# A planner's costs for crossbar transposes beside loads, and the order that it makes, in an attention and gated feed-forward kernel

## The chip, the cores and the metric

The kernel runs on one core of one Trainium2 chip. The metric is the device time of one execution in microseconds (us), from the runs shown below. The engines that matter are TensorE (PE in the profile, with its weight loads as PEld), VectorE (DVE), ScalarE (ACT), GpSimd (POOL), which here only issues loads, and SyncE (SP), which issues crossbar transposes and stores.

## The reference

```python
def _attn_ref(q, k, v):                       # each 8 x 12 x 448 x 64
    scale = 1.0 / np.sqrt(q.shape[-1])
    scores = scale * np.matmul(q, k.transpose(0, 1, 3, 2))
    attn = np.maximum(scores, 0.0) ** 2 / S
    return np.matmul(attn, v)

def _moe_ref(x, w_gate, w_val, w_out):        # 3584 x 768; 768 x 1536 twice; 1536 x 768
    gate = np.maximum(x @ w_gate, 0.0)
    val = x @ w_val
    return gate * val @ w_out
```

The attention's heads are joined to a 3584 x 768 matrix, which is the feed-forward's `x`. Inputs and output are float32; the kernel computes in bfloat16.

## The kernel before

The work goes by batch (8, named b) and by group of four heads (3 to a batch, named g), 24 groups in all. A group's queries and keys are loaded to `raw`, its values to `vv`, both by POOL (L393, `dma_in`). They have to be transposed to `qkT`. For the first two batches TensorE does that (L508, L515, L555). For the other 18 groups VectorE copies `raw` into `perm`, of which there is one buffer (L579), and SP issues two crossbar transposes `perm` to `qkT` (L585), a pair for each group. Then TensorE forms the scores (L653), ScalarE or VectorE applies relu (L664, L666) and square (L676, L678), and TensorE multiplies by the values (L695). The results of a batch are `xT`.

The feed-forward of the first two batches is plain (L760 for gate and value). From the third batch on, two batches go together by Strassen's scheme with seven products for eight (L869), and the output products do so for all batches (L984). Their sums are formed on VectorE and ScalarE (among them L816 to L822, L897, L935, L974). Stores go out from SP, the last ones from ACT too (L956).

While TensorE waits for the first loads it runs products whose result nobody reads ("filler", L1138).

The order of every engine's queue is made by the class `Planner` and the function `plan` when the program is built. The planner keeps a time for each engine, each buffer and two DMA queues (loads, transposes), and repeatedly lets the operation start that it thinks can start first. Each engine then executes its queue in order, waiting by semaphore where an input is late. The planner's costs therefore change no instruction, only the order and which of ScalarE and VectorE does an operation that both can do. Three strings hold the result of a search: `PE_ORDER` (how attention, in lower case, and feed-forward, in upper case, are merged on TensorE), `LOAD_ORDER` (POOL's loads) and `AHEAD` (by how many tenths of a microsecond each operation of the other engines is preferred or put back).

The costs of the two DMA queues are these. A load arrives `TO_LOAD` after its issue, needs its own work (`op.load`) at full rate, and ends `LOADED` after that. A pair of transposes likewise has `TO_TURN`, `TURN` and `TURNED`. While both queues hold something, each gets half of the rate (L135 to L164, `advance` and `transfer`). An operation of TensorE or another engine that needs a transposed tile is kept `LATE[0]` behind its landing; a buffer that a DMA reads is free `LATE[1]` behind its end. Operations of VectorE and ScalarE that read a load are kept `MARGIN` behind it.

Of the kernel before, what the change touches and what calls it, by code (L numbers as in the profile page):

```python
# [15 lines left out]
class Res:  # L16


    def __init__(self, n):
        self.free = {i: 0.0 for i in range(n)}  # L20
# [21 lines left out]
class Op:  # L42


    def __init__(self, engs, emit, deps=(), alloc=(), reads=(), mode=None, grp=None):
        self.engs, self.emit = engs, emit
        self.deps, self.alloc, self.reads = list(deps), list(alloc), list(reads)
        self.mode, self.grp = mode, grp
        self.load = self.land = 0.0
        self.kind = self.behind = None  # L50
        self.xbar = 0
        self.start = self.end = self.eng = None
        for b in self.reads:
            b.readers += 1


class Planner:
    NOUT = 8
    SWITCH = 0.1
    BIAS = 0.2  # L60
    MARGIN = 1.0
# [43 lines left out]
    def ready(self, op):  # L105
        r = 0.0
        for d in op.deps:
            if d.end is None:
                return None
            if d.eng != "PE" or "PE" not in op.engs:  # L110
                r = max(r, d.end + (self.LATE[0] if d.xbar else 0.0))
        for b in op.alloc:
            p = b.pick(self.now(op))
            if p is None:
                return None
            r = max(r, p[0])
        return r

    def best(self, op):
# [4 lines left out]
        for e, (occ, busy) in op.engs.items():  # L124
            if e in ("DVE", "ACT"):
                r = max([r] + [d.end + self.MARGIN for d in op.deps if d.load])
            s = max(r, self.t.get(e, 0.0))
# [4 lines left out]
                c = (f, s, e)  # L132
        return c[1], c[2], r

    def advance(self, t):  # L135

        a, b = self.queues
        while self.dma_t < t and (a or b):
            rate = 0.5 if a and b else 1.0
            d = min(min(q[0][1] for q in (a, b) if q) / rate, t - self.dma_t)  # L140
            self.dma_t += d
            for q, post in ((a, self.LOADED), (b, self.TURNED)):
                if q:
                    q[0][1] -= d * rate
                    if q[0][1] < 1e-6:
                        q.pop(0)[0].end = self.dma_t + post
        self.dma_t = max(self.dma_t, t)

    def transfer(self, queue, op, arrival, work):


        self.advance(arrival)
        self.queues[queue].append([op, work])
        a, b = ([list(x) for x in q] for q in self.queues)
        t = self.dma_t
        while a or b:
            rate = 0.5 if a and b else 1.0
            d = min(q[0][1] for q in (a, b) if q) / rate
            t += d
            for q, post in ((a, self.LOADED), (b, self.TURNED)):  # L160
                if q:
                    q[0][1] -= d * rate
                    if q[0][1] < 1e-6:
                        q.pop(0)[0].end = t + post  # L164

    def commit(self, op, s, e):
        assert op.behind is None or op.behind.start is not None
# [28 lines left out]


PE_ORDER = (
    'aadccabacbcadafgabaedabbafecaaCacaFFABAacbaAAieadbbJJIIbaaIHAFGahebccbJJHcaaHFICBDgaadbCFbaEDABBBabfeBANCccLBa'
    'aIIGDAABegcdaBIAEbbaHACCgbbdaDDFcaaAAAbgbdAAdaACBbaAAhcbbAaabBCBAaaCBAebbaCBbaaEAGBBcDBFAEBAADCBAGAAHAEBBCBAAB'  # L200
    'DfaAADaaCABAcBBABaaACAAacbabDADAEEAABABADAabEDDBACEAAACCbaBABABbbCBaaABDAbbEAAabAGAebaAACEAabEEFABfbBEgaAAabhc'
    'BBcgbCCaDAecdABbaaAAAAaaacBAADaaDBDACAAEBCAcbDAHBAGAABAAAacAGAAaabBAAAAABAAAbbaCAAIAAAbbaDAAbcCAAAHBAHacAAFbaB'
    'DEAgbaABCCBACBABBDABAedCBAbaaAFCAAAAAeaaaICcaAAAbaABAaaaaBBcaaCEIACaBEJAKAADBAACABAAABAAAAAABAAAAAABAAAADADHCB'
    'DCBICHABCFBHACAFEBEHBABCAEGBBDBBDCCECAAAGBABBABBBCGEAABBCBCCBABBABBBA'
)
LOAD_ORDER = (
    'aaaabacebaacbacaabaaabadhcegaadeedabaaacahbgcabgeefdaddafccaabdacadmacehaadadmaaiabbdfhiadcaaabccgladdigaaabcb'
    'aaaabaa'
)
AHEAD = (  # L210
    'mlmmmolklollknklnlmomknomlmmmmnlllomnollmmomkommlmkmmmmjmkknqkkhnmnliilnnommmokoljkkopnmnojokmioinklrnkohplrmi'
    'hjolnponoeilomskljrjkunmqpnmjjnmjijjmomolsmokiiijnhpotkioksohoolopnjirmompnjppplhmnjqgjpoqqmnjkmpljmlkklkoqkoj'
    'noookqplkjlllgnoqntlloopmpopnmjlnoomonlmpnqmqklmlnkkknojpsonpgmnmkkhnmommnpjmlmjnlhompplnmnookmlmoqkkkkolmoopj'
    'ooplpmnoomomnnolmmmmkmmmmmmlmmmnnknnnpllmlonlonlmmkgnmqlkpmniuilqnlliruojriqkoosmnpqophgpnitnjinonoqpnplnmmmll'
    'loknokmlmmjnpopnojmnmljnliqimnenkoojmkgjdoonlmnnrtnorhogrmppnijllliomrorkigpjnpjkmqoonohloqlmqohpnpmpmikklooin'
    'ltlvnnnomkmmunipomhnnmjjgmmmphgjnloilsogplmomplqiolkkkqhnmkngojmojkllmnohmjjkpklnkrnkkklomlilmnkjknjknokqlnlll'
    'kjjlpnmrljklmmniqnpqilknmlklmnllolojonnimnpliljkionjoilklkiimmkrloonniolnlnkmnonnklmlklkmlnnnmmmmmmmmmmmmmmmmm'
    'mmomnmklkkolmlommolnnnnmlmloljmlpikogimnolpolqjjnimlngpijlpmkonknlmjleklpsjnoqnqlqkmilrsmmoomjojmjhppsjrpppllq'
    'horhmnknqrpknjpmpnokjjppnhilpmhomiphpmpojqokkkpoonkoihjkmojnljklipnqlnnksnklmkirqmpmklhgknllfrlgqkjknmlfjnrrmp'
    'slmrmnnnikmonninkjmmmqjlikpqqmnjohpijopklkn'  # L220
)

# [75 lines left out]
def kernel(  # L298
# [28 lines left out]
    OH = d_model // 2  # L327
# [21 lines left out]
    wo = pool.tile([128, 2, 2, FH, OH], BF16, name="wo")  # L349
# [39 lines left out]
    others, pool_ops = [], []  # L389


    def dma_in(dst, src, n_desc, us, deps=(), alloc=()):
        op = Op({"POOL": (0.5 + 0.0004 * n_desc,) * 2}, lambda: nc.gpsimd.dma_start(out=dst(), in_=src),  # L393
                deps=deps, alloc=alloc)
        op.load = us
        pool_ops.append(op)
        return op

    wg_op, wv_op, wo_op = {}, {}, {}

    def load_gv(m0, m1):

        cols = slice(m0 * 128, m1 * 128)
        for ops, sb, w in ((wg_op, wg, moe_w_gate), (wv_op, wv, moe_w_val)):
            src = w.rearrange("(kd p) f -> p kd f", p=128)
            op = dma_in(lambda sb=sb: sb[:, :, cols], src[:, :, cols], 768,
                        1.075 * (m1 - m0) + (0.0 if wv_op or sb is wv else 0.65))
            for m in range(m0, m1):
                ops[m] = op

    def load_out(par, hf):
        src = moe_w_out.rearrange("(g par p) m -> p par g m", p=128, par=2)
        wo_op[(par, hf)] = dma_in(lambda: wo[:, par, hf], src[:, par, :, hf * OH:(hf + 1) * OH], 768, 3.0)

    class Quad:
        pass
# [730 lines left out]
    def load_quad(b, g):  # L1147
        load_qk(b, g)
        load_v(b, g)
# [3 lines left out]
    for x in Planner.ORDER:  # L1153
        if x in "VL":
            for g in range(NQ):
                load_v(0, g) if x == "V" else late_q(g)
        elif x in quad_of:
            load_quad(*quad_of[x])
        elif x in out_of:
            load_out(*out_of[x])  # L1160
        elif x == "6":
            load_gv(1, 2)
        elif x == "0" and "6" in Planner.ORDER:
            load_gv(0, 1)
        else:
            load_gv(2 * int(x), 2 * int(x) + 2)
# [83 lines left out]
```

## Time and profile before

| | |
|---|---|
| timed runs, us | 407.9, 406.82, 404.08 (median 406.82) |
| profiled execution, us | 403.85 |
| its span, first to last instruction, us | 402.1 |
| granted TensorE clock | 0.998 |
| TensorE busy | 390.4 us, 97% |
| VectorE, ScalarE, GpSimd busy | 81%, 66%, 19% |
| HBM read, written | 47.19 MB, 11.01 MB |

The profile shows one execution. Its busy times say how full each engine is; the waits of TensorE say what it stood for; the chain that ended last says which work set the end; the timeline shows single places. Wherever a view gives "to landing", it is the time from the issue of a DMA to the last of its data. Times in a view count from the span's start.

### The profile page before, as it was taken

What the parts mean: (1) busy time and instruction counts of PE and PEld (TensorE: products, weight loads), DVE (VectorE), ACT (ScalarE), POOL (GpSimd) and SP (SyncE); (2) the same over time, 40 slices, a digit from 0 to 9 for tenths busy, and PEclk for the clock granted to TensorE, in tenths of its full rate; (3) what the DMA queues carried; (4) which work ended last, traced back from release to release, by engine and by line L of the source; (5) the groups of instructions that cost most, each with busy time, mean ns of one, the idle gap of its engine ahead of it and who ended that gap; (6) DMA issues with size and microseconds to landing.
All of it is one profiled execution on the core that took longest, in us unless ns stands there. A gap on an engine that the chain in (4) does not pass through costs nothing.

```text
span 402.1 us, 8702 instructions
## 1 busy us (share of the span) xinstructions
PE 390.4 (97%) x3472; PEld 209.0 (52%) x3472; DVE 325.2 (81%) x570; ACT 267.1 (66%) x395; POOL 75.7 (19%) x121
## 2 busy tenths in 40 slices
PE   7899998999999999999999999999999999999995
PEld 4577554455455554444455544444455555555563
DVE  4998784999899869988998978998889858768661
ACT  3888884768987637957859874588688853233231
POOL 8845541032202110212102220310100000000000
PEclk9999999999999999999999999999999999999999
DMA  8999999987999585266567993761513320000245
GB/s 112 191 197 199 199 182 198 151 124 98 116 156 166 120 152 82 41 93 102 81 101 136 195 196 50 111 91 30 76 36 82 80 59 0 2 0 2 60 120 138
DMA packets 77305, 43.44 MB, mean 108 GB/s; under 512 B 40912, under 2 KB 77264, under 8 KB 77264
## 3 DMA queue, kind: packets, MB, share of 16 engines
q0 software_dynamic: 34896, 23.60, 42.2%
q1 hardware_dynamic: 42048, 18.89, 25.4%
q8 instruction: 27, 0.44, 0.4%
q10 hardware_dynamic: 320, 0.39, 0.3%
q14 instruction: 14, 0.11, 0.1%
HBM read 47.19 MB, written 11.01 MB: 145 GB/s over the span
## 4 chain that ended last, share of the span: by engine, by line
PE 88%; DMA 9%; issue 1%; POOL 1%; ACT 1%; DVE 0%; SPq 0%; DVEq 0%; POOLq 0%
PE ps L869 35%; PE ps L984 24%; PE ps L760 12%; PE ps L653 9%; PE ps L695 7%; DMA qkT<-perm 6%; DMA gvT<-in_k_dram 1%; DMA vv<-in_v_dram 1%; POOL gvT L393 1%; PE ps L555 1%; ACT at L664 0%; DVE g L935 0%; ACT qkT L481 0%; DVE o L974 0%; PE ps L1138 0%
## 5 line engine op out<-in xcount | busy, mean ns | idle before, releaser
L664 ACT ACTIVATE at<-ps 128x896 bf16<-128x896 f32 (+4 forms) x124 | 108.2, 903 | 23.6 <-PE ps L653 23.3
L816 ACT COPY f<-ps 128x448 f32<-128x448 f32 x97 | 51.2, 532 | 49.1 <-PE ps L869 38.7
L678 DVE TENSOR_TENSOR at<-at 128x896 bf16<-128x896 bf16 (+4 forms) x108 | 64.0, 608 | 10.3 <-ACT at L664 8.9
L676 ACT ACTIVATE at<-at 128x896 bf16<-128x896 bf16 (+2 forms) x63 | 59.1, 952 | 1.7 <-DVE at L666 0.8
L666 DVE TENSOR_SCALAR at<-ps 128x896 bf16<-128x896 f32 (+3 forms) x47 | 50.6, 1076 | 4.1 <-PE ps L653 2.8
L653 PE MATMUL ps<-qkT 64*64 64x448 bf16 (+2 forms) x756 | 49.5, 337 | 1.8 <-DMA qkT<-perm 1.7
L869 PE MATMUL ps<-sx,wv 128*128 128x448 bf16 x216 | 51.1, 353 | 0.0
L869 PE MATMUL ps<-xT,gvT 128*128 128x448 bf16 x216 | 50.4, 353 | 0.0
L869 PE MATMUL ps<-xT,wg 128*128 128x448 bf16 x216 | 49.4, 353 | 0.8 <-DVE g L935 0.8
L393 POOL DMA_DIRECT2D vv<-in_v_dram x44 | 26.6, 609 | 119.0 <-PE ps L653 105.3
L869 PEld LDWEIGHTS <-gvT 128*128 128x128 bf16 x324 | 30.9, 98 | 30.7 <-issue 2.9
L984 PEld LDWEIGHTS <-sh 128*128 128x128 bf16 x312 | 29.8, 98 | 22.2 <-issue 1.9
L984 PEld LDWEIGHTS <-hT 128*128 128x128 bf16 x270 | 25.3, 98 | 20.6 <-issue 4.2
L984 PE MATMUL ps<-wo,hT 128*128 128x384 bf16 x192 | 35.6, 326 | 0.0
L695 PE MATMUL ps<-at,vv 64*64 64x448 bf16 (+2 forms) x700 | 34.0, 328 | 0.8 <-ACT at L664 0.5
L974 DVE SCALAR_TENSOR_TENSOR o<-ps,f 128x384 f32<-128x384 f32 x41 | 22.6, 555 | 13.9 <-PE ps L984 8.2
L653 PEld LDWEIGHTS <-qkT 64*64 64x64 bf16 x756 | 19.1, 105 | 26.1 <-issue 20.1
L818 ACT ACTIVATE f<-ps 128x384 f32<-128x384 f32 x39 | 19.1, 492 | 19.8 <-PE ps L984 17.8
L869 PEld LDWEIGHTS <-wg 128*128 128x128 bf16 x216 | 20.6, 98 | 21.4 <-issue 3.2
L760 PE MATMUL ps<-xT,wg 128*128 128x448 bf16 (+2 forms) x180 | 31.5, 316 | 0.0
L760 PE MATMUL ps<-xT,wv 128*128 128x448 bf16 (+2 forms) x180 | 31.3, 316 | 0.0
L869 PEld LDWEIGHTS <-wv 128*128 128x128 bf16 x216 | 20.2, 98 | 21.3 <-issue 3.7
(71 smaller groups left out, 489.9 us busy)
## 6 DMA issues: line engine op xcount, KB each, us to landing
out_dram<-o SPq DMA_DIRECT2D x108, 96.0 KB, 2.2
vv<-in_v_dram POOLq DMA_DIRECT2D x44, 112.0 KB, 5.3
raw<-in_k_dram POOLq DMA_DIRECT2D x18, 224.0 KB, 4.9
raw<-in_q_dram POOLq DMA_DIRECT2D x18, 224.0 KB, 6.1
wo<-in_moe_w_out_dram POOLq DMA_DIRECT2D x4, 576.0 KB, 15.1
wv<-in_moe_w_val_dram POOLq DMA_DIRECT2D x5, 384.0 KB, 9.7
wg<-in_moe_w_gate_dram POOLq DMA_DIRECT2D x5, 384.0 KB, 9.6
gvT<-in_k_dram POOLq DMA_DIRECT2D x6, 224.0 KB, 7.6
```

Of the source, the lines that this page charges most:

```text
L393: op = Op({"POOL": (0.5 + 0.0004 * n_desc,) * 2}, lambda: nc.gpsimd.dma_start(out=dst(), in_=src), deps=deps, alloc=alloc)
L653: nc.tensor.matmul(banks()[64 * j:64 * j + 64, z, h2], lhsT=self.k_of(j, h2, k), rhs=self.q_of(j, h2), start=True, stop=True)
L664: nc.scalar.activation(self.at_of(i, m), banks(), AF.Relu)
L666: nc.vector.tensor_scalar_max(self.at_of(i, m), banks(), 0.0)
L676: nc.scalar.activation(a, a, AF.Square)
L678: nc.vector.tensor_tensor(a, a, a, ALU.mult)
L695: nc.tensor.matmul(ps[64 * h2:64 * h2 + 64, ps2.idx + j, :n], lhsT=st.v_of(j, h2, c), rhs=self.at_of(c)[64 * j:64 * j + 64, 0, h2], start= ...
L760: nc.tensor.matmul(ps[:, pb.idx, z * n:(z + 1) * n], lhsT=w[:, kd, fc], rhs=xT_t[xbuf[b].idx][:, kd, cols], start=(kd == 0), stop=(kd == K ...
L816: nc.scalar.copy(dst, src)
L869: nc.tensor.matmul(ps[:, pb.idx, :S], lhsT=w(g)[:, fc], rhs=rhs, start=start and g == 0, stop=stop and g == KH - 1, skip_group_check=True)
L974: op = Op({"DVE": V384}, lambda: nc.vector.scalar_tensor_tensor(o_t[ob.idx], ps[:, pb.idx, :OH], float(out_scale), f_t[fb.idx][:, :OH], AL ...
L984: nc.tensor.matmul(ps[:, pb.idx, :OH], lhsT=lhs(kf), rhs=rhs(kf), start=start and kf == 0, stop=kf == FH - 1, skip_group_check=True)
```

## The change

Four things in the planner, and the three strings.

- Loads and transposes that are under way together no longer get half each. Each load has a `share`, the part of the rate that a transpose gets beside it: 0.25 for queries, keys and the gate and value weights, 0.19 for the output weights, 0.5 for values.
- The six constants of the two DMA queues are set anew.
- What waits for a transposed tile is kept 2.0 instead of 1.0 us behind its planned landing, and TensorE, which was not kept off a load, is kept 0.3 us behind it; `MARGIN` goes from 1.0 to 1.5.
- `advance` and the look-ahead in `transfer` are merged into `flow`.

```diff
-    MARGIN = 1.0
-    LATE = (1.0, 1.0)
-    TO_LOAD, LOADED = 2.25, 0.8
-    TO_TURN, TURNED, TURN = 1.8, 0.55, 4.05
+    MARGIN = 1.5
+    LATE = (2.0, 1.0, 0.3)
+    TO_LOAD, LOADED = 2.35, 0.95
+    TO_TURN, TURNED, TURN = 1.7, 0.8, 3.65
...
-                r = max(r, d.end + (self.LATE[0] if d.xbar else 0.0))
+                r = max(r, d.end + (self.LATE[0] if d.xbar else self.LATE[2] if d.load else 0.0))
...
-            rate = 0.5 if a and b else 1.0
...
+    def rates(self, a, b):
+        if not (a and b):
+            return 1.0, 1.0
+        share = a[0][0].share
+        return 1.0 - share, share
+
+    def flow(self, a, b, t, until):
+        while t < until and (a or b):
+            rates = self.rates(a, b)
+            d = min([q[0][1] / r for q, r in zip((a, b), rates) if q] + [until - t])
+            t += d
+            for q, r, post in zip((a, b), rates, (self.LOADED, self.TURNED)):
+                if q:
+                    q[0][1] -= d * r
                     if q[0][1] < 1e-6:
                         q.pop(0)[0].end = t + post
+        return t
...
-    def dma_in(dst, src, n_desc, us, deps=(), alloc=()):
+    def dma_in(dst, src, n_desc, us, deps=(), alloc=(), share=0.25):
...
-        wo_op[(par, hf)] = dma_in(..., 768, 3.0)
+        wo_op[(par, hf)] = dma_in(..., 768, 3.0, share=0.19)
...
-            st.v_ops.append(dma_in(lambda j=j: st.vv()[64 * j:64 * j + 64], src, 128, 0.58,
+            st.v_ops.append(dma_in(lambda j=j: st.vv()[64 * j:64 * j + 64], src, 128, 0.58, share=0.5,
```

The strings begin like this, before and after; they differ over most of `AHEAD`, the first four rows of `PE_ORDER` and the second half of `LOAD_ORDER`'s first row.

```diff
-    'aadccabacbcadafgabaedabbafecaaCacaFFABAacbaAAieadbbJJIIbaaIHAFGahebccbJJHcaaHFICBDgaadbCFbaEDABBBabfeBANCccLBa'
+    'aaceccaacbcbacaeibbeccabaaecabAAacaFAccACaaabgcbaaNKJKATAHaaaJCICcebeJEEIbbFbaaGADFafabBABEabaBBAAabfeAKTLabKK'
...
-    'aaaabacebaacbacaabaaabadhcegaadeedabaaacahbgcabgeefdaddafccaabdacadmacehaadadmaaiabbdfhiadcaaabccgladdigaaabcb'
+    'aaaabacebaacbacaaeccbaaidceokbdacgeeafafiaegeahcdgdfdcacabdddbddaalllacacccaaalaiccbddagaabddahdeacanlcahjbhca'
```

Both programs have the same number of instructions of each kind that computes on TensorE except the filler (3472 and 3471 products with it), the same 117 loads, 36 transposes and 112 stores.

More of the change, by code (lines that the diff above doesn't have):

```diff
@@ L48, in __init__ @@
         self.mode, self.grp = mode, grp
-        self.load = self.land = 0.0
+        self.load = self.land = self.share = 0.0
         self.kind = self.behind = None
@@ L133, in best, with transfer @@
         return c[1], c[2], r
-    def advance(self, t):
-        a, b = self.queues
-        while self.dma_t < t and (a or b):
-            rate = 0.5 if a and b else 1.0
-            d = min(min(q[0][1] for q in (a, b) if q) / rate, t - self.dma_t)
-            self.dma_t += d
-            for q, post in ((a, self.LOADED), (b, self.TURNED)):
-                if q:
[L144 to L162, printed above, removed]
+    def rates(self, a, b):
[9 more added lines that the diff above has]
+            for q, r, post in zip((a, b), rates, (self.LOADED, self.TURNED)):
+                if q:
+                    q[0][1] -= d * r
                     if q[0][1] < 1e-6:
                         q.pop(0)[0].end = t + post
+        return t
+    def transfer(self, queue, op, arrival, work):
+        self.dma_t = max(self.flow(*self.queues, self.dma_t, arrival), arrival, self.dma_t)
+        self.queues[queue].append([op, work])
+        self.flow(*([list(x) for x in q] for q in self.queues), self.dma_t, 1e9)
     def commit(self, op, s, e):
@@ L198 @@
 PE_ORDER = (
-    'aadccabacbcadafgabaedabbafecaaCacaFFABAacbaAAieadbbJJIIbaaIHAFGahebccbJJHcaaHFICBDgaadbCFbaEDABBBabfeBANCccLBa'
[L200 to L203, printed above, removed]
+    'aaceccaacbcbacaeibbeccabaaecabAAacaFAccACaaabgcbaaNKJKATAHaaaJCICcebeJEEIbbFbaaGADFafabBABEabaBBAAabfeAKTLabKK'
+    'CCGbaCDCAhecddHBBbbaDGACafbdaDDbaaFCAAbgbdAAacACBbaAAhcbbCaabABBbaDAAAebbaCcaaBIABCBcBABEEBAADCBAGAAHAEBBCBAAB'
+    'DfaAADaaCABAcBBABaaACBAacbabDAAFCAACBCFCHBAEBCcBAAACbaAACAGAabbBABaaBCADAecbEACAaAFebaBACEAabEEFABfaFgaaABbdiA'
+    'caCeaGBABBecdCAcbaAAAABfabaAEKADBAQAAEAAACBAAAbaDBAbbBDABAdaGCAAaabAAECAaBABBAAbaAIBAAbbaDAAbcAAJBCBAHAAFacBFA'
+    'CbaACBACAAgbaAECEACBAedCAAbaaAFCAAAAAeaaaICcaAAbaAABAaaaaBBcbaCJEACaBEJAKAADBAACABAAABCBBBACBCDCBAABAAAADADHCB'
     'DCBICHABCFBHACAFEBEHBABCAEGBBDBBDCCECAAAGBABBABBBCGEAABBCBCCBABBABBBA'
@@ L206 @@
 LOAD_ORDER = (
-    'aaaabacebaacbacaabaaabadhcegaadeedabaaacahbgcabgeefdaddafccaabdacadmacehaadadmaaiabbdfhiadcaaabccgladdigaaabcb'
-    'aaaabaa'
+    'aaaabacebaacbacaaeccbaaidceokbdacgeeafafiaegeahcdgdfdcacabdddbddaalllacacccaaalaiccbddagaabddahdeacanlcahjbhca'
+    'bdaabba'
 )
 AHEAD = (
-    'mlmmmolklollknklnlmomknomlmmmmnlllomnollmmomkommlmkmmmmjmkknqkkhnmnliilnnommmokoljkkopnmnojokmioinklrnkohplrmi'
-    'hjolnponoeilomskljrjkunmqpnmjjnmjijjmomolsmokiiijnhpotkioksohoolopnjirmompnjppplhmnjqgjpoqqmnjkmpljmlkklkoqkoj'
@@ L218 @@
-    'mmomnmklkkolmlommolnnnnmlmloljmlpikogimnolpolqjjnimlngpijlpmkonknlmjleklpsjnoqnqlqkmilrsmmoomjojmjhppsjrpppllq'
-    'horhmnknqrpknjpmpnokjjppnhilpmhomiphpmpojqokkkpoonkoihjkmojnljklipnqlnnksnklmkirqmpmklhgknllfrlgqkjknmlfjnrrmp'
+    'mlmmmolklollknkknkmplknmkjnnnmolnlmmnqlkmoqokonmjkmkmokimmkloohjrnlghglokjjklmmqngmhtlhprneoficpkmjjsfnnpwrtpg'
+    'arogqkpqrainsvngkgjgjzorsopgfnlrljmjoprmpskjjdbhgmmttnkmrlwpellhjpnjkqpqrlnlqlskbktfsijmkppnnjgkqllpmfhrkrlloh'
+    'qtorjsllojjfkgpprlrhkmnppqlqoljlpmlnnrlooorlohholmjnlpofrwqmnfloogmisphjnnnhijlkqilojnokqkiomoorllqohglslmmmhn'
@@ new lines @@
+    'smlowookpgijmqkqmpjjrflkinkjiimhqpqommkljnnonompjslgpppjhornftieqplmirwlkthrihsurmosnrjfnmgvnhjnsrqoslhomntmol'
+    'mvliqeknljmkmqsqlhmpsilnjklimmapnrqlnmdjgokqqnnorpigtjqitsoomkggjihpntqtqnenkpkiiuoposrepoqlnthjmkplplkkkkmsio'
+    'irqvpnimlemgqspnnnbtukjkinnqjhgkkmqcisldokjnmqknkmklklofqnlpfnknqhlmknomgljilsiknjsnijlipknjmmpkjnrjlmqepmnflh'
+    'ghknornoimjpoljkpmoqjiorpofnlplnnkrbmqpgompihkkkisqinkijffhlqpurmqpovfmgmgnnoorlompkoljpnnlqomlkopskhoihmkmnok'
+    'onoiooemgipikpjimfknjomqmoipontjlkopgooljjlpmrjkifmhohpdjloliqokpmrligmhsufqrtosfrhrggpronqqkkmjmmlsqqlqtqoooq'
@@ L220 @@
+    'gmqikmklrspkmjrmonpihjponiinpmhmogphpmpnjqmklkoonlipgilmkmjnkjingpnqkmojsnklmkjrqmpmklhgknllfrlgqkjknmlfjnrrmp'
     'slmrmnnnikmonninkjmmmqjlikpqqmnjohpijopklkn'
@@ L389 @@
     others, pool_ops = [], []
-    def dma_in(dst, src, n_desc, us, deps=(), alloc=()):
+    def dma_in(dst, src, n_desc, us, deps=(), alloc=(), share=0.25):
         op = Op({"POOL": (0.5 + 0.0004 * n_desc,) * 2}, lambda: nc.gpsimd.dma_start(out=dst(), in_=src),
                 deps=deps, alloc=alloc)
-        op.load = us
+        op.load, op.share = us, share
         pool_ops.append(op)
@@ L412, in load_out @@
         src = moe_w_out.rearrange("(g par p) m -> p par g m", p=128, par=2)
-        wo_op[(par, hf)] = dma_in(lambda: wo[:, par, hf], src[:, par, :, hf * OH:(hf + 1) * OH], 768, 3.0)
+        wo_op[(par, hf)] = dma_in(lambda: wo[:, par, hf], src[:, par, :, hf * OH:(hf + 1) * OH], 768, 3.0, share=0.19)
     class Quad:
```

5 lines of the change are left out of this document (removed).

## Prediction, made before the changed kernel ran

> **What bounds the kernel now.** I read the page's busy times first, then TensorE's waits, then the chain that ended last, and last the timeline at the two places where the chain leaves TensorE.
>
> ```profile
> PE 390.4 (97%) x3472; PEld 209.0 (52%) x3472; DVE 325.2 (81%) x570; ACT 267.1 (66%) x395; POOL 75.7 (19%) x121
> ...
> PE 88%; DMA 9%; issue 1%; POOL 1%; ACT 1%; DVE 0%; SPq 0%; DVEq 0%; POOLq 0%
> ```
>
> TensorE is busy for 390.4 of 402.1 us. Of the 11.7 us left, some 4.5 lie behind its last product (rows below). A change of order adds or removes no product of the result, so it can work only on the idle time, on the filler products and on changes of matrix shape.
>
> ```profile
> PE ps L653 <- DMA qkT<-perm: 1.7, 1, 1.7
> PE ps L1138 <- DVE woT L1125: 1.4, 1, 1.4
> PE ps L869 <- DVE g L935: 0.8, 1, 0.8
> PE ps L508 <- DMA gvT<-in_q_dram: 0.8, 2, 0.4
> PE ps L555 <- issue: 0.6, 1, 0.6
> PE ps L515 <- issue: 0.6, 1, 0.6
> ```
>
> These are TensorE's own waits. The first is a wait for a crossbar transpose and is the target of the change; the third will turn out to be a transpose too. The 1.4 us is the start of the program, the rest belongs to the first 35 us.
>
> ```profile
> 51.67 14.19 DMA qkT<-perm
> 65.91 0.38 PE ps L653 x4
> ...
> 231.53 9.19 DMA qkT<-perm
> 240.90 0.48 issue
> 241.38 0.63 DVE g L935
> 242.05 1.29 PE ps L869 x6
> ...
> 325.45 44.29 PE ps L869 x234
> ...
> 372.26 25.36 PE ps L984 x156
> 397.65 0.56 DVE o L974
> ```
>
> This is the chain in order of time (start, us, what). It leaves TensorE for a transpose twice. From 325 us on it is products alone, at 44.29/234 = 0.189 us for 448 columns and 25.36/156 = 0.163 us for 384: nothing to gain there. The tail from 397.65 to 402.1 holds an add and the last stores, which the change leaves alone.
>
> ```profile
> 49.57 0.62 DVE L579 COPY perm<-raw 128x1792 bf16<-128x1792 bf16 x1
> 50.29 5.89 SPq L585 DMA_TRANSPOSE qkT<-perm  x2
> 65.91 0.38 PE L653 MATMUL ps<-qkT 64*64 64x448 bf16 x4 [1.65 <-DMA qkT<-perm]
> ...
> 240.84 0.63 DVE L579 COPY perm<-raw 128x1792 bf16<-128x1792 bf16 x1 [2.05 <-DMA qkT<-perm]
> 241.38 0.62 DVE L935 CUSTOM_DVE_ANT_0 g<-ps,f 128x448 bf16<-128x448 f32 x1
> 242.05 0.73 PE L869 MATMUL ps<-xT,wg 128*128 128x448 bf16 x3 [0.84 <-DVE g L935]
> ```
>
> The timeline of both places. VectorE copies a group into `perm`, SP issues two transposes, and 15.6 us later (50.29 to 65.9) the scores start, 1.65 us late. At 240.84 it is the single `perm` buffer: VectorE stands for 2.05 us until the pair before has left it, the addition behind it (L935) comes late, and TensorE waits 0.84 us.
>
> ```profile
> DMA to landing us min/median/max: 11.3/12.7/14.2
> ...
> DMA to landing us min/median/max: 10.3/10.6/10.8
> ...
> DMA to landing us min/median/max: 3.5/3.6/3.7
> ```
>
> The two transposes issued at 50 to 52 us, at 68 to 70 and at 155 to 157, where no load runs beside them. SP issues the second of a pair 1.3 us behind the first, so a pair needs about 5.0 us alone (1.3 + 3.7) and 15.6 beside loads. An equal share for both would make it 10. So the planner before was wrong at this place, and a share near a quarter, as the change gives it, is nearer the row.
>
> ```profile
> q0 software_dynamic: 34896, 23.60, 42.2%
> q1 hardware_dynamic: 42048, 18.89, 25.4%
> ```
>
> The Trainium skill, page "DMA: Bandwidth & Descriptors", section "Queues, rings and completion order", says that each DMA engine takes turns between its queues packet by packet. By that rule a pair beside loads has a share of its own packets' size over both: 449 of 449 + 676 bytes (18.89 MB over 42048, 23.60 MB over 34896), 40%, and takes 12.5 us; the trace has 15.6, so the measurement decides and the rule would understate the leads needed. The sum below does without it.
>
> **The change part by part.** The constants alter no instruction; only the three strings and what the planner makes of them do. I counted in the order of the engines how much TensorE work stands between the last product that VectorE waits for ahead of a copy into `perm` and the first scores that read the transposed tile.
>
> First pair. Before: 140 products (28 scores, 28 of L695, 48, 18 and 18 of L760 with 448, 256 and 192 columns). After: 210 (52, 56, 60, 30 and 12). With 0.189, 0.11 and 0.083 us for the widths of L760 (by columns from the 0.189), and the next rows for the others, that is 15.7 and 21.6 us.
>
> ```profile
> 83.59 0.50 PE ps L653 x8
> 84.09 1.32 PE ps L695 x28
> ```
>
> Eight scores in 0.50 us, 28 products of L695 in 1.32. The lead grows by 5.9 us where 1.65 us were missing: this wait goes, **-1.65 us** (bounds -1.65 and 0, the latter if its loads get as much longer).
>
> Pair at 230 us. Between the product ahead of its copy and that ahead of the next copy stand 78 products before, 82 after, of which 12 and 30 are 448-column ones, 18 and 12 those of L984, 20 and 12 scores, 28 and 28 L695: 7.8 and 9.7 us. The gap grows by 1.9 us where VectorE stood for 2.05: **-0.84 us** (bounds -0.84 and 0).
>
> Later pairs. Their waits were nil, so longer leads there are worth nothing. Some leads shrink: the fourth pair's from 18.4 to 14.5 us by the same count.
>
> ```profile
> 94.42 3.04 SPq L585 DMA_TRANSPOSE qkT<-perm  x2
> ...
> DMA to landing us min/median/max: 6.6/7.5/8.4
> ...
> 105.52 0.57 PE L653 MATMUL ps<-qkT 64*64 64x448 bf16 x8
> ```
>
> The second of this pair, issued at 95.7, landed at 104.1 (+8.4) with 1.4 us to spare. Should the loads beside it stay, the shrunk lead would cost 3.9 - 1.4 = 2.5 us. But in POOL's new queue the loads that this copy lets go stand behind a V load that itself waits for products of L695, so that the pair has few loads beside it, as at 155 us: I take 0, bounds 0 and +2.5.
>
> Second copy into `perm`. It stands 15.6 us of products behind the first (14.5 before), and the copy and the first pair need 0.6 + 15.6. Before, TensorE's own stop of 1.65 us hid this. VectorE will stand for about 0.6 us, and by the place at 240 us (2.05 us there, 0.84 at TensorE) plus what hangs behind it I take **+0.5** (bounds 0 and +2).
>
> ```profile
> L1138 PE MATMUL ps<-woT 128*128 128x410 bf16 x12 | 3.8, 495 | 1.4 <-DVE woT L1125 1.4
> ...
> 5.00:34.00 29.00, 25.68 (x600) 18.61 (x601) 24.17 (x43) 23.60 (x36) 19.72 (x31) 1.00 1.38 188
> ```
>
> Start. The first 17 loads on POOL keep their order; behind them a key piece and two narrow weight pieces move ahead of two wide ones. Filler products stand only where the planner has nothing for TensorE: 34 with 12,888 columns before, 33 with 13,355 after. At 3.8 us for 12 of 410 columns the 467 more are **+0.4 us** (bounds 0 and +2: TensorE was idle for 3.3 of the 29 us of the second row, and a start held back more could add more than half as much again).
>
> Changes of shape. Runs of products of one shape go from 148 to 153. A visit of eight scores takes 0.50 us where two passes of 0.189 would be 0.38, so a visit (two changes) costs 0.12; five changes are **+0.3 us** (bounds 0 and +0.6).
>
> Sum: -1.65 - 0.84 + 0.5 + 0.4 + 0.3 = -1.3 us. The profiled execution took 403.85 us (its span 402.1 and 1.75 around it), so 402.6 after.
>
> The three timed runs are 404.08, 406.82 and 407.9; the profiled one lies below all. What made the others longer no trace shows. The leads say what would: scores that started 0.05 us behind their tile wait for the whole of any slower loading. With 5.9 us more of lead this goes, but slower loads also hold up the first 35 us, which no lead covers. I let half of the 3 us between profile and median stay: 402.6 + 1.5 = **404.1 us**.
>
> **The rivals.**
>
> A. All of the spread was late transposes, and the runs after come out like the profile: 402.6 less up to 1 if the start costs nothing, so 401.6. For it: the 1.4 us to spare at 105 and the 0.05 at 65.9, both eaten by a pair a tenth longer. Against: 5 to 34 us is loads and short products, where leads do nothing.
>
> B. The wait moves to the fourth pair. The fourth pair loses its 2.5 us, and the runs keep the whole 3 us of spread: 402.6 + 2.5 = 405.1 profiled, 408 in the median; with half of the 2.5, 406.8, no change. For it: TensorE at 97% leaves little to win. Against: no load need run beside the fourth pair.
>
> C. The second pair meets the output weights.
>
> ```profile
> wo<-in_moe_w_out_dram POOLq DMA_DIRECT2D x4, 576.0 KB, 15.1
> ...
> DMA to landing us min/median/max: 13.7/15.1/20.0
> ...
> 68.55 4.64 SPq L585 DMA_TRANSPOSE qkT<-perm  x2
> ```
>
> Before, these four loads ran mostly beside the first pair and the 18 us behind it; in the new program the second copy follows behind the third of them, so its pair shares with them, and four smaller loads come behind the last. Its lead is 23.8 us of products (18.5 before, of which 83.5 - 68.55 = 15.0 were left when SP issued; of the first pair's 15.7, 65.9 - 1.65 - 50.3 = 14.0): 1.7 to 3.5 pass before the issue, so 20 to 22 are left. At a quarter of the rate it needs 15.6; at the 0.19 that the change gives beside these loads, 15.6 x 0.25 / 0.19 = 20.5. From a pair of 22 us on it decides, and each us more is a us of TensorE; the slowest of these loads took 20.0 to land, and the four small ones behind it (672 KB, a little more than one of them) would make that some 26, 4 to 5 us late: 402.6 + 5 + 1.5 = 409, slower than before. For it: the lead is hardly longer than the need. Against: the second pair took 1.3 + 10.3 us with the last of the same loads still under way.
>
> D. That nothing is changed is not possible: the queues differ from the first filler on.
>
> **How the numbers follow.** Forecast 0.45, A 0.26, B 0.16, C 0.13. The likeliest case's own range is 402.6 (nothing left of the spread) to 405.6 (all of it). For 8 in 10 the range takes in most of A and B and the near half of C: 401.0 to 408.5. About 1% either way (402.75 and 410.9) is what a measurement of this kernel can tell from no change. Faster by more: nearly all of A and a little of the forecast, 0.29. Slower by more: the far part of C and some unseen start, 0.08. Within: 0.63.
>
> **What would show it right or wrong.** Right: no row of TensorE waiting for `qkT<-perm`; L869's wait for L935 gone; the first pair still at 13 to 17 us from issue to landing; TensorE busy within 1 us of 390.4; the last product near 396.3. Wrong at the first term: the row stays, with another pair in it. Wrong at the start: more than 0.5 us of new waits on L508, L515, L555 or L695 below 35 us, or filler well above its time before. C: a wait of L653 near 80 to 87 us. Wrong on the spread: timed runs still 3 us above the profile.

## The result, and the profile after

The changed kernel takes 403.62 us in the median of 20 runs, the kernel before 405.98 in 20 runs: 0.9952 of it, with a 95% interval of 0.9928 to 0.9975. The profiled execution took 403.12 us where before took 403.85. The runs also lie closer together: the middle half of them from 403.3 to 404.9, before from 404.4 to 407.8. Ratios here and below leave out runs over 1.5% above the fastest of the same kernel beside them, among them two of the twelve with the first copy early.

First the head of the page after, and the engines' shares of its chain.

```profile
span 401.3 us, 8739 instructions
PE 391.8 (98%) x3471; PEld 208.7 (52%) x3471; DVE 323.7 (81%) x563; ACT 273.6 (68%) x402; POOL 75.6 (19%) x121
PE 74%; DMA 16%; issue 6%; POOL 2%; DVE 1%; SPq 0%; DVEq 0%; POOLq 0%
```

TensorE is busy for 1.4 us more, and the span is 0.8 us shorter: 2.2 us less idle time. The chain has more DMA in it, 16% for 9%, yet the kernel is faster: the chain follows whatever came last, however little too late it came. What counts is what TensorE stood for:

```profile
PE ps L1133 <- DVE woT L1120: 1.4, 1, 1.4
PE ps L648 <- ACT at L659: 0.9, 1, 0.9
PE ps L648 <- DVE at L661: 0.9, 2, 0.8
PE ps L503 <- DMA gvT<-in_q_dram: 0.4, 1, 0.4
PE ps L979 <- DVE f L817: 0.3, 1, 0.3
```

Line numbers are five lower than before (L648 is L653 of before, L574 the copy into `perm`, L580 the transposes). No row has `qkT<-perm`, and none has L935's new number: both waits of the prediction are gone. How the first scores stand now, from TensorE's timeline, and three of VectorE's copies into `perm`:

```profile
65.49 0.38 PE L648 MATMUL ps<-qkT 64*64 64x448 bf16 x4
```

```profile
61.39 0.63 DVE L574 COPY perm<-raw 128x1792 bf16<-128x1792 bf16 x1 [1.59 <-DMA qkT<-perm]
203.62 0.63 DVE L574 COPY perm<-raw 128x1792 bf16<-128x1792 bf16 x1 [1.00 <-DMA qkT<-perm]
240.75 0.63 DVE L574 COPY perm<-raw 128x1792 bf16<-128x1792 bf16 x1 [0.41 <-DMA raw<-in_q_dram]
```

The scores follow without a gap. VectorE stands for the single `perm` at two other copies, 1.59 and 1.00 us. The transposes of the first, second and fourth copy (rows of L580, issue to landing):

```profile
DMA to landing us min/median/max: 9.1/11.2/13.3
...
DMA to landing us min/median/max: 10.9/12.7/14.5
...
DMA to landing us min/median/max: 3.5/3.7/3.8
```

The pairs of the first two ran beside loads, and with the 1.3 us between their issues took 14.7 and 15.7 us. The fourth, with nothing beside it, took 5.1.

Where TensorE's idle time is, by stretches (length, then TensorE's busy time). Before, then after:

```profile
5.00:36.00 31.00, 27.68 (x626) 20.36 (x626) 26.04 (x46) 25.38 (x38) 21.72 (x33) 1.00 1.39 189
64.00:90.00 26.00, 24.35 (x203) 12.30 (x202) 21.72 (x29) 17.64 (x25) 4.87 (x8) 1.00 1.09 152
225.00:247.00 22.00, 21.16 (x164) 10.40 (x162) 19.11 (x37) 16.07 (x25) 3.94 (x7) 1.00 1.03 173
```

```profile
5.00:36.00 31.00, 28.10 (x630) 20.02 (x629) 25.36 (x45) 26.86 (x41) 20.92 (x32) 1.00 1.40 191
64.00:90.00 26.00, 25.74 (x215) 12.57 (x214) 24.10 (x31) 18.85 (x26) 4.24 (x7) 1.00 1.15 158
125.00:225.00 100.00, 99.45 (x804) 50.01 (x803) 87.55 (x154) 72.04 (x104) 16.05 (x27) 1.00 0.69 109
225.00:247.00 22.00, 22.00 (x167) 11.32 (x169) 18.31 (x35) 16.03 (x26) 4.68 (x8) 1.00 0.91 157
```

From 64 to 90 us the idle time fell from 1.65 to 0.26 us, from 225 to 247 from 0.84 to nothing, in the start from 3.32 to 2.90. The stretch in the middle lost 0.55 (before: nothing).

### The profile page after: what moved, and what is told of

Read it like the earlier page. It is cut to its first block, busy times and chain, and to the rows that moved or that the text cites. A ratio compares the mean times of both kernels' runs of the same rounds, so it can differ in the third digit from the quotient of the medians.

```text
span 401.3 us, 8739 instructions
## 1 busy us (share of the span) xinstructions
PE 391.8 (98%) x3471; PEld 208.7 (52%) x3471; DVE 323.7 (81%) x563; ACT 273.6 (68%) x402; POOL 75.6 (19%) x121
## 4 chain that ended last, share of the span: by engine, by line
PE 74%; DMA 16%; issue 6%; POOL 2%; DVE 1%; SPq 0%; DVEq 0%; POOLq 0%
PE ps L864 36%; PE ps L979 18%; PE ps L755 8%; PE ps L648 6%; PE ps L690 5%; DMA qkT<-perm 5%; DMA wg<-in_moe_w_gate_dram 5%; DMA vv<-in_v_dram 3%; DMA gvT<-in_v_dram 2%; DMA gvT<-in_k_dram 1%; POOL vv L388 1%; DVE perm L574 0%; POOL gvT L388 0%; POOL raw L388 0%; DVE at L661 0%
## 5 line engine op out<-in xcount | busy, mean ns | idle before, releaser
L659 ACT ACTIVATE at<-ps 128x896 bf16<-128x896 f32 (+3 forms) x119 | 105.5, 911 | 21.2 <-PE ps L648 20.6
L811 ACT COPY f<-ps 128x448 f32<-128x448 f32 x101 | 53.1, 533 | 46.8 <-PE ps L864 31.7
L671 ACT ACTIVATE at<-at 128x896 bf16<-128x896 bf16 (+2 forms) x72 | 66.8, 938 | 2.3 <-DVE at L661 1.2
L673 DVE TENSOR_TENSOR at<-at 128x896 bf16<-128x896 bf16 (+3 forms) x99 | 59.0, 612 | 5.5 <-ACT at L659 4.5
L661 DVE TENSOR_SCALAR at<-ps 128x896 bf16<-128x896 f32 (+4 forms) x52 | 54.5, 1050 | 6.3 <-PE ps L648 6.0
L648 PE MATMUL ps<-qkT 64*64 64x448 bf16 (+2 forms) x756 | 50.3, 338 | 2.0 <-ACT at L659 0.9
L979 PEld LDWEIGHTS <-sh 128*128 128x128 bf16 x312 | 29.2, 98 | 23.9 <-issue 4.7
L979 PEld LDWEIGHTS <-hT 128*128 128x128 bf16 x270 | 25.6, 98 | 19.9 <-issue 3.4
L979 PE MATMUL ps<-wo,hT 128*128 128x384 bf16 x192 | 35.4, 326 | 0.0
L648 PEld LDWEIGHTS <-qkT 64*64 64x64 bf16 x756 | 18.9, 105 | 27.7 <-issue 23.8
L969 DVE SCALAR_TENSOR_TENSOR o<-ps,f 128x384 f32<-128x384 f32 x41 | 22.5, 554 | 12.6 <-PE ps L979 7.9
```

The costliest lines, as they stand in the source:

```text
L648: nc.tensor.matmul(banks()[64 * j:64 * j + 64, z, h2], lhsT=self.k_of(j, h2, k), rhs=self.q_of(j, h2), start=True, stop=True)
L659: nc.scalar.activation(self.at_of(i, m), banks(), AF.Relu)
L661: nc.vector.tensor_scalar_max(self.at_of(i, m), banks(), 0.0)
L671: nc.scalar.activation(a, a, AF.Square)
L673: nc.vector.tensor_tensor(a, a, a, ALU.mult)
L811: nc.scalar.copy(dst, src)
```

## The experiments

Most of them move single instructions in a finished queue: the planner's list is taken apart by engine, a copy into `perm` is moved by so many places of VectorE's queue (copies are counted from 0, negative is ahead), and every other queue keeps its order. Each ratio is to runs of the kernel before taken beside that kernel. The theories were: **W**, that the two waits that transposes cause are what the change won; **S**, that it was won in the first 35 us; later **V**, on why the runs of before lie apart; **P**, on what the place of a copy costs; **F**, on costs and strings.

### The change's two gains alone, in the kernel before

```diff
+    def edit(queues):
+        dve = queues["DVE"]
+        copies = [o for o in dve if o.kind == "perm"]
+        put_back(dve, copies[0], -2)      # first copy early, and both
+        put_back(dve, copies[14], 2)      # later copy back, and both
```

The first copy early: 

> The kernel before with one instruction moved: the first copy into perm stands two places earlier in VectorE's queue (ahead of an hT product and a relu), so that the first pair of transposes is issued some 2.5 us earlier. Theory W (the waits that transposes cause are what the change won): the 1.65 us wait of L653 near 66 us is gone, the lateness after it is carried to the end, profiled time lower by 1.2 to 1.7 us; the median of the runs lower by 1.5 to 2.5 us, since slower runs lost more there. Rival S (the change won in the first 35 us, a wait taken away is given back by later waits): profiled time and median within 0.5 us of before. Rival L (the pair's end is set by the loads beside it, not by its issue): the pair takes 2 us longer, the wait stays over 1 us, nothing won.

The later copy back: 

> The kernel before with one instruction moved: the copy into perm near 241 us stands two places later in VectorE's queue, behind the two additions that waited behind it. Theory W: VectorE no longer stands 2 us there, TensorE's 0.84 us wait for L935 is gone, profiled time lower by 0.8 to 1.3 us, median likewise. Rival S: within 0.5 us of before, the time comes back before 325 us.

Both: 

> Both moves in the kernel before. Theory W: the two gains add, 2.0 to 3.0 us in the profiled time, which would be below the changed kernel's (403.1), because the old order has fewer changes of shape and no late second copy; the runs lie closer together than before's, as far apart as the changed kernel's. Rival S: no better than one per cent in a thousand, and the runs as far apart as before's.

Against 405.63 us of the kernel before (35 runs):

| | median, us | ratio, 95% interval | middle half of the runs, us |
|---|---|---|---|
| before | 405.63 | | 404.3 to 407.5 |
| first copy early | 405.17 | 0.9974, 0.9937 to 1.0011 | 402.3 to 407.2 |
| later copy back | 404.44 | 0.9970, 0.9938 to 1.0002 | 403.8 to 405.1 |
| both | 403.33 | 0.9942, 0.9913 to 0.9971 | 402.8 to 404.2 |

Two instructions, moved by two places each, give in the median what the whole new order gives. Alone, the later copy gives about half of it (1.2 us) and the first copy 0.5 us, with intervals that just reach no change. So W holds for the medians of both moves and of the later copy. For the first copy alone S gave the right size, and the profiles fell short of W in all three: 403.39, 403.70 and 403.44 us are 0.46, 0.15 and 0.41 us below before's, where W had 1.2 to 1.7, 0.8 to 1.3 and 2.0 to 3.0. With the first copy early, its wait is gone, but this profile has another copy that stands:

```profile
81.74 0.63 DVE L615 COPY perm<-raw 128x1792 bf16<-128x1792 bf16 x1 [2.02 <-DMA qkT<-perm]
```

It is the third. The second pair took 14.6 us here (11.55 in the profile of before), and 1.6 of the 1.7 us won came back at 80 to 85 us. In the profile with both moves the 1.7 us were kept. But TensorE came out of the start 0.55 us later than in before's profile, and it stood for 1.2 us between 225 and 247 us, where the pair took 12.6 us (10.5 in before) and the later copy still stood for 0.62. The last column shows the other half: with the later copy moved the runs lie together, with the first alone they lie at least as far apart as before.

### The same kernels in another execution

Before, once more: 

> The kernel before once more, for the profile of another execution. Theory V (its executions differ because pairs beside loads take from 10 to 15 us, and a late one is a wait where little time is to spare): the same instructions, but pairs whose time from issue to landing differs by 1 us or more from the first profile's, and TensorE's time at equal work differs at those places and not elsewhere. Rival O (the start or another stage makes the difference): TensorE's time differs by more than 0.5 us before 45 us or behind 260 us.

It took 406.39 us, 2.54 more than the first profile. TensorE's waits, and the stretches:

```profile
PE ps L869 <- DVE g L935: 2.0, 1, 2.0
PE ps L653 <- DMA qkT<-perm: 1.5, 1, 1.5
...
PE ps L515 <- issue: 1.3, 1, 1.3
```

```profile
5.00:36.00 31.00, 26.94 (x622) 20.03 (x623) 25.77 (x46) 25.08 (x38) 21.91 (x34) 1.00 1.39 191
64.00:90.00 26.00, 24.46 (x203) 12.29 (x202) 21.60 (x30) 17.44 (x25) 4.85 (x8) 1.00 1.07 145
225.00:247.00 22.00, 19.33 (x152) 9.32 (x150) 16.68 (x32) 14.06 (x21) 4.12 (x7) 1.00 1.18 162
```

Of the 2.5 us, 1.8 lie between 225 and 247 us (idle 2.67 for 0.84) and 0.7 in the start; when the start of the n-th product is compared instead, 2.36 and 0.2, with nothing in between or behind. Of the 2.36 us, 1.2 are the copy's longer stop (first row, 2.0 for 0.84). The other 1.16 came ahead of it, at 231 to 235 us, in the products of L695 and ahead of L869. The pair at 230 us, and the copy behind it, in the first execution and in this one:

```profile
DMA to landing us min/median/max: 6.8/8.0/9.2
raw<-in_q_dram POOLq DMA_DIRECT2D x2, 224.0 KB, 6.8
240.84 0.63 DVE L579 COPY perm<-raw 128x1792 bf16<-128x1792 bf16 x1 [2.05 <-DMA qkT<-perm]
```

```profile
DMA to landing us min/median/max: 9.9/10.8/11.7
raw<-in_q_dram POOLq DMA_DIRECT2D x2, 224.0 KB, 9.7
243.39 0.63 DVE L579 COPY perm<-raw 128x1792 bf16<-128x1792 bf16 x1 [3.18 <-DMA qkT<-perm]
```

The same transfers in the same order took 10.5 us once and 13.0 the other time, and the loads beside them slowed down as well: the DMA as a whole served this stretch at 173 and 162 GB/s. What makes it slower no view shows. V held for the place: the two executions of before differ where a slow pair has nothing to spare. But half of the difference there is not the pair's own stop.

The changed kernel, once more: 

> The changed kernel once more, for the profile of another execution. Theory V: it differs from the first at the copies that stood there (61, 138, 204 us) and nowhere else, by less than 1 us, since no pair beside loads has a thin margin left. Theory S (the change's start is better, and not by chance of one execution): TensorE's time at equal work at 36 us is again 1 us or more ahead of that of both executions of before.

It took 404.82 us. Nothing is lost between 225 and 247 us here either, the copy at 62 us stands 1.59 us again, and the first 31 us look so:

```profile
5.00:36.00 31.00, 27.23 (x624) 19.45 (x623) 24.82 (x44) 26.40 (x39) 20.67 (x31) 1.00 1.39 188
```

An idle time of 3.77 us in the start, against 2.90 in the first profile and 3.32 and 4.06 in the two of before. By these profiles S fell: the start differs by as much between executions as between kernels. V fell here too, with its 1 us and with the places: the two profiles of the changed kernel differ by 1.7 us. The start has 0.87 of it by idle time. By the start of the n-th product, 1.0 us lies between 85 and 117 us, where the sixth copy stands for 1.35 us behind a pair of 10.5 us (0.38 and 9.5 in the first profile). So thin margins were left.

One thing these profiles can't weigh is TensorE's clock. The mean granted clock is known for each timed run of the experiments and of the changed kernel. Of 77 runs of before, the 22 with 0.998 or more took 404.4 us in the median and 405.9 at most; the other 55 took 406.9 in the median. Of the changed kernel's 20 runs, 18 had 0.998 or more and the others 0.997. Both profiles of before had 0.998 and 0.999, so no trace of it shows a run with the lower clock. Two profiles with before's order in the start show a place where the clock fell. This is the later copy alone, ahead of the fall and in it (the clock is the last but two of the columns):

```profile
17.80:21.20 3.40, 1.88 (x69) 1.31 (x58) 3.15 (x7) 2.88 (x5) 2.03 (x4) 1.00 1.49 196
21.20:24.60 3.40, 3.27 (x61) 2.84 (x62) 2.06 (x3) 2.26 (x4) 0.83 (x1) 0.50 1.58 191
```

The clock is 0.50 for 3.4 us, though TensorE's longest stop there was 1.1 us; with both moves it is the same from 22.3 us on. At 28 us these two were 1.1 and 1.4 us later than before's first profile, at 42 us still 0.2 and 0.55. In no profile of the changed kernel, or of one made from it, did the clock fall in the start. So a part of the gain and of before's spread may belong to the start after all; no run separates it. The later copy's move brought the runs together although 11 of its 12 runs had a clock below 0.998.

### Six places instead of two

> The kernel before with two of VectorE's copies into perm moved: the first two places ahead, and the one that stands at 240 us six places back (in e3 it was two), where its own pair has 19 us to spare. Theory V (the runs lie apart because the pair ahead of that copy takes 10.5 to 13 us and the first pair 15 to 16, and each us of it is a us of TensorE): the copy stands no more whatever the pair takes, so the median is 402.3 to 403.3 and all runs lie within 3 us. Rival O (what makes the runs differ is elsewhere): the median is e3's 403.3 or above and the runs lie 4 us apart or more, as those of e3 did.

404.03 us, ratio 0.9955 (0.9921 to 0.9989), runs from 402.84 to 405.8, their middle half 403.3 to 404.3. In its profile the pair at 230 us took 13.3 us, and the copy behind it (at 243.74) no longer stood. But the kernel is no faster than with two places. TensorE's waits, and VectorE's copies at 244 us:

```profile
PE ps L732 <- DVE hT L807: 0.8, 2, 0.6
PE ps L906 <- DVE g L934: 0.7, 1, 0.7
...
PE ps L906 <- DVE xT L750: 0.5, 1, 0.5
```

```profile
243.74 0.62 DVE L615 COPY perm<-raw 128x1792 bf16<-128x1792 bf16 x1
...
249.47 0.63 DVE L615 COPY perm<-raw 128x1792 bf16<-128x1792 bf16 x1 [1.00 <-DMA qkT<-perm]
```

The copy that was put back six places is now too near to the next one, which stands 1.00 us for the pair between them (4.9 us), and TensorE waits 0.7 us for the sum behind that copy (L934). The 0.5 us, at 235 us, come after VectorE stood for stores of `o`, 0.78 and 0.94 us at 230 us: in a slow stretch these are late as well. The first row is the third copy's stand near 80 us again, 2.14 us here. Of V, the runs' spread came as expected; the median did not: six places made a new wait, and with two the copy's stand had cost TensorE only 0.3 us in the profile with both moves.

### What the place of a copy costs, in the changed kernel

```diff
+        put_back(dve, copies[0], 6)       # both kernels
+        put_back(dve, copies[1], 6)       # the second kernel alone
```

The first copy alone: 

> The changed kernel with one instruction moved: VectorE's first copy into perm stands six places further back, so that some 6.7 us of the products between it and the first scores go, where the first pair had 4.2 us to spare. All other queues keep their order. Theory W (the longer lead is worth what the wait cost): the scores wait 1 to 2.5 us for qkT<-perm near 65 us, the second pair follows later and has 5.7 us to spare less that: the profile takes 1 to 2.5 us more than 403.1, the median 404.6 to 406. Rival G (a wait that is taken away is given back behind it, and one put in costs nothing): 403.2 to 404.1, with the wait in the profile but the end where it was.

Both: 

> The changed kernel with VectorE's first and second copies into perm both six places further back, so that the first pair's lead to its scores is cut as in e8, but the distance between the two copies is kept. Theory P (what the place of a copy costs is set by its distance to the next copy into the single perm buffer, measured against the time of the pair between them; the lead to the scores counts by the microseconds by which it is too short): the second copy stands under 2.5 us instead of 8.4, the first scores wait for qkT<-perm for 1.5 to 3 us near 66 us, and the kernel takes 404.5 to 407. Rival Q (a first copy at 52 us costs what it cost in e8, whoever waits): TensorE stops for 6 us or more in all between 60 and 75 us and the kernel takes 411 to 413.

One copy moved by six places makes the kernel some 9 us slower than the changed one, 412.80 us (ratio to before 1.0177, 1.0150 to 1.0205): both theories fell. The wait of the scores that was expected isn't there. TensorE, VectorE and the granted clock:

```profile
69.61 3.68 PE L792 MATMUL ps<-xT,wv 128*128 128x256 bf16 x12 [6.49 <-DVE at L698]
```

```profile
67.93 0.63 DVE L610 COPY perm<-raw 128x1792 bf16<-128x1792 bf16 x1 [8.36 <-DMA qkT<-perm]
```

```profile
63.00:69.50 6.50, 0.11 (x1) 0.00 (x0) 1.57 (x2) 0.69 (x2) 0.00 (x0) 0.85 1.29 195
69.50:71.50 2.00, 1.90 (x8) 1.13 (x8) 1.97 (x5) 0.00 (x0) 0.00 (x0) 0.50 1.31 204
```

The copy that was moved now stands eleven places of VectorE's queue ahead of the second one instead of seventeen, and there is one `perm`. So the second copy holds VectorE for 8.36 us until the first pair (15.1 us) has left it. The relus of scores behind it come late, and TensorE stops for 6.5 us. Its clock is then granted at half, and the twelve products that took 1.95 us in the kernel below take 3.68.

With both copies moved it is 408.08 us (1.0074, 1.0040 to 1.0109):

```profile
63.92 1.95 PE L792 MATMUL ps<-xT,wv 128*128 128x256 bf16 x12
69.32 0.38 PE L684 MATMUL ps<-qkT 64*64 64x448 bf16 x4 [3.45 <-DMA qkT<-perm]
```

```profile
66.00:69.30 3.30, 0.00 (x0) 0.00 (x0) 0.61 (x1) 0.00 (x0) 0.00 (x0) 1.00 1.28 195
69.30:71.50 2.20, 2.18 (x41) 1.24 (x42) 1.42 (x3) 1.31 (x2) 0.17 (x1) 1.00 1.32 205
```

```profile
69.40 0.63 DVE L610 COPY perm<-raw 128x1792 bf16<-128x1792 bf16 x1 [2.79 <-DMA raw<-in_k_dram]
```

Now it is the scores that wait, 3.45 us, and the second copy stands 2.79. The view names a load for that, but this load had landed at 49.97 us; what left `perm` 0.12 us before the copy, at 69.28, was the first pair (15.6 us). P's mechanism is borne out, its sizes were somewhat too small (1.5 to 3 us, under 2.5, 404.5 to 407), and Q fell. The copy's distance to the next copy and its lead to the scores are two prices, and the first is the higher one.

In the first of these two kernels 8.2 of the 8.6 us in the span are accounted for: 6.49 of the stop and 1.73 of the half clock over these twelve products. The Trainium skill, page "TensorE: Matmul & The Clock Gate", section "Part 1: The HAM clock gate", says that the clock falls to half after an idle window of about 3.4 us, whose start doesn't follow the program. These rows agree: half after 6.5 us, full after 3.45. The falls near 21 us in the two profiles above do not, since TensorE was busy for 1.88 of the 3.4 us ahead of one of them; there the measurement decides.

### Costs without strings, strings without costs

```diff
-    MARGIN = 1.0                          # first kernel: before with all of
-    LATE = (1.0, 1.0)                     # the change but the three strings
+    MARGIN = 1.5
+    LATE = (2.0, 1.0, 0.3)
...
-        share = a[0][0].share             # second kernel: the changed kernel
+        share = 0.5                       # with the queue costs of before
```

Costs alone: 

> The kernel before with the new costs of the planner (MARGIN, LATE, the transfer constants, the shares by kind of load) and its three old strings. Theory F (the strings are worth something only with the costs they were searched with; a planner that knows transposes better gives no gain by itself): the old strings' choices fall on other times, so the order is a poorer one: 406 to 411 us, with new waits of TensorE of 0.5 us or more at several places from 35 us on, whether or not the first scores' wait of 1.65 us is gone. Rival K (the better knowledge of transposes is the gain): the first scores' wait is gone and the time is that of the change, 402.5 to 404.5 us.

The strings with the queue costs of before: 

> The changed kernel with its new strings, MARGIN and LATE, but with equal shares for a transpose and a load beside it and the six transfer constants of before. Theory F: the new strings lose their fit as well: 405 to 410 us, with transposes late again, since the planner believes a pair beside loads to take 10 us where the trace shows 15: a wait for qkT<-perm of 1 us or more at one of the first three pairs. Rival S2 (the new strings carry the gain, the shares none of it): within 1 us of the changed kernel's 403.6, no wait for a transpose over 0.3 us.

415.21 us (1.0236, 1.0200 to 1.0271) and 410.89 us (1.0148, 1.0108 to 1.0187): F held for both in kind, with times past its ranges by 4.2 and 0.9 us. The old strings under the new costs give several new waits:

```profile
PE ps L510 <- issue: 2.5, 1, 2.5
PE ps L648 <- DMA qkT<-perm: 2.0, 1, 2.0
```

The new strings under the old costs lose their time between 95 and 130 us (5.84 us idle, the changed kernel none), and not to transposes: F expected a wait for one there, and the row is another.

```profile
PE ps L648 <- ACT at L659: 4.1, 4, 1.0
```

Scores wait for a relu on ScalarE. The strings choose by the planner's own times; with other times the same letters are another order. Whether a new search under the old costs would have found as much no run shows.

### The changed kernel with its two standing copies moved

```diff
+        put_back(dve, copies[1], 2)
+        put_back(dve, copies[12], 2)
```

> The changed kernel with two instructions moved: the second copy into perm (near 61 us, where VectorE stands 1.59 us) and the thirteenth (near 204 us, 1.00 us) stand two places later in VectorE's queue. Theory W: the losses of 0.5 us at TensorE near 61 us and 0.6 near 202 us go, so 0.7 to 1.1 us below the changed kernel, profiled near 402.2, median near 402.7. Rival S: same as the changed kernel within 0.4 us.

403.29 us, 0.9939 (0.9906 to 0.9971); profiled 402.17, the shortest of all. W's profile came out; its median of 402.7 did not, and S's (within 0.4 us of the changed kernel) did. The copies at 62.5 and 204 us stand no more:

```profile
62.47 0.62 DVE L610 COPY perm<-raw 128x1792 bf16<-128x1792 bf16 x1
204.05 0.62 DVE L610 COPY perm<-raw 128x1792 bf16<-128x1792 bf16 x1
```

It has the lowest median measured, but its lead over the changed kernel, 0.9939 against 0.9952, is smaller than either interval.

## Why the prediction was right or wrong

The forecast was 404.1 us, within 1% of before; measured are 403.62 and 0.5% less. That it came so near is in part luck, since two errors cancel. The profiled execution was to take 402.6 with the last product near 396.3, and took 403.12 with the last one ending at 397.07, 0.5 us too long. The median was to lie 1.5 us above the profile and lay 0.5 above it. By the steps:

- **First pair, -1.65 us: right.** The wait is gone, and in the kernel before with the first copy alone moved, 1.7 us were won at that place. What the step didn't say is that before's third copy takes it back where the second pair takes 14.6 us. The changed order keeps 20.4 us between its second and third copy (61.39 to 81.80), and there nothing came back.
- **Pair at 230 us, -0.84: right in kind, sized from one execution.** In the other the same wait was 2.0 us, and the stretch around it lost 2.67 in all.
- **Later pairs, 0: right for the fourth, wrong for another.** The fourth pair had nothing beside it, as the step said, and took 5.1 us; rival B fell with that. But the step looked at leads to scores alone. The copy at 203.62 stood 1.00 us for the pair ahead of it (7.45 us), TensorE lost 0.3 us there (L979), and moving that copy, in the last experiment, won 0.5 us at that place.
- **Second copy, +0.5: the stand was mis-sized, the price less so.** VectorE stood 1.59 us, not 0.6, but TensorE lost only 0.27 us there. The prediction took the stand from the pair's time beside a lead counted in products, and that lead was 1.3 us shorter.
- **Start, +0.4: not settled.** Idle time of 2.90 and 3.77 us against 3.32 and 4.06 is no difference that two profiles of each can show, and the clock in the start is open too.
- **Changes of shape, +0.3: not settled.** TensorE's busy time rose by 1.4 us, where "within 1 us" was expected. The scores' group has 50.3 us for 49.5; but kernels with before's own TensorE order showed 390.4 to 392.1 in all.
- **Half of the spread stays: too much, and in the wrong place.** Before, the median lay 2.1 us above the profile (405.98 and 403.85; 3.0 by the three runs known then), after, 0.5 (403.62 and 403.12). The prediction blamed the first scores' 0.05 us of lead. But moving that copy left the runs as far apart as before, and moving the later one brought them together. The 0.84 us stop at 240 us, which the sum took as a fixed price, was 2.0 in the other profile. What made the longest runs of before, up to 409.4 us, no trace shows.
- **Rival C fell.** The second pair took 15.7 us beside the output weights, not 20.5 or 22: the smaller share that the change gives beside these loads was not what the chip gave. It had 5.7 us to spare, like the first, which had 4.2.
- **Rival A fell** at 401.6 us: not all of the spread was transposes, as the start of the second execution after shows.
- **The rule of turns was tried with the wrong packets.** The 449 bytes that gave 40% and 12.5 us are the mean of all of queue q1 over the whole execution, stores included. The two queues of before while the first pair moved, from 54.3 to 65.5 us (packets, MB, busy share):

```profile
q0 software_dynamic: 1931, 1.53, 92.2%
q1 hardware_dynamic: 1852, 0.46, 37.1%
```

The packets went nearly one for one, and the pair, with packets of 0.46 MB over 1852 or some 250 bytes, had 23% of the bytes. So the row bears out the rule that the prediction set aside, and the share of a quarter with it. Beside the output weights, from 66 to 77.4 us after, it was the same: 1854 packets and 0.46 MB to 1944 and 1.52.

## What to carry to other kernels

Where one buffer passes work from an engine to a slow transfer, compare the distance between two fills with the transfer's longest time, not only the lead to the reader: the engine that fills it stands with all that is queued behind, here 8.4 us for six places. A profile is one execution; a wait that has just come out at 0.8 us behind a transfer under contention can be 2 us in the next, so price it by the transfer's range. A share between two queues is read from the packets of the stretch in question, not from a queue's mean over the execution. And a searched order belongs to the costs it was searched with: look for the few instructions that carry its gain and move them by hand before searching anew.

## What the runs showed of the hardware

- The same pair of transposes in an unchanged order took 10.5 and 13.0 us in two executions of one kernel, with loads beside it at 6.8 and 9.7 us; the pair at 155 us, with nothing beside it, took 5.0 in each.
- The first pair, beside loads, took 14.7 to 16.2 us in every profile; the changed kernel's second, beside output weights, 15.7 and 15.8.
- While the first pair of before moved, its packets (250 bytes in the mean) and those of the loads (790 bytes) went nearly one for one, 1852 and 1931, which left it 23% of the bytes.
- A stop of TensorE of 6.5 us cost a further 1.7 us on the twelve products behind it, by a granted clock of 0.50; one of 3.45 us left the clock at 1.00. In two profiles the clock was 0.50 for 3.4 us from 21 or 22 us on, with no stop there longer than 1.2 us.
